# Gathering the experts' rows as quarter rows and turning them on VectorE

## The chip, the cores and the metric

The kernel runs on one core of one Trainium2 chip. The metric is device time in microseconds (us) of one execution. The profile calls TensorE's matmuls PE and its weight loads PEld, VectorE DVE, ScalarE ACT, GpSimd POOL and SyncE SP.

## The reference

Sliding-window attention (8 batches, 8 heads, 576 positions, head size 64, window 64) is followed by a mixture of experts in which each row uses one expert. A local gate decides whether a row takes its own best expert or keeps that of the row before it.

```python
# attention output, laid out as x: (8, 576, 512)
logits = np.einsum('bsd,de->bse', x, w_gate)          # 8 experts
local_gate = 1.0 / (1.0 + np.exp(-np.einsum('bsd,de->bse', x, w_local).squeeze(-1)))
...
            fresh_e = int(np.argmax(logits[b, s]))
            if s == 0 or local_gate[b, s] < 0.5:
                e = fresh_e
            else:
                e = prev_e if prev_e >= 0 else fresh_e
...
            h = np.maximum(x[b, s] @ w1[e], 0.0)      # 512 -> 1024
            out[b, s] = p[e] * (h @ w2[e])            # 1024 -> 512
```

All data are 32-bit floats; p is the softmax of the logits.

## The kernel before, in words

**Attention** (line 168 on) works through nine chunks of 512 rows, four pairs of heads each. The finished rows go by DMA to a table in DRAM, `xs` (line 106), one row of 512 values and 16 more columns (`PITCH`) that hold the row's weight p. The **Router** (line 702 on) sorts the 4608 rows by expert in two parts while other work runs: `first` for the rows of the first part, `second` for all. Its results are index tables: `idx` and `gx` say for every place in a block which row stands there, `ej` which expert a block has. The weights p go into the last columns of `xs` in `weigh`.

**Experts** (line 1131 on) then works block by block. A slot is 128 places. A *big* block has two slots (256 rows), a *single* block one, a *half* block 64 rows and a *quarter* block 32. The order is fixed in `run` (line 1498): three big blocks of the first part (-1, -2, -3), then

0, 1, S, 2, Q, 3, S, 4, 5, S, 6, Q, 7, S, 8, 9, H, 10, 11, 12, H

where a number is a big block, S a single, H a half and Q a quarter one. For each block:

- `rows` (line 1144) gathers its rows: for each slot one indirect DMA on GpSimd's queue takes 128 rows of 528 values from `xs` into a tile `xg` (line 1162). `weights` (line 1170) loads the expert's w1 and w2 by SP into a ring of four tiles. Both are done two blocks ahead.
- `turn` (line 1189) brings the 512 features onto the partitions: PE transposes each slot in four 128x128 pieces into PSUM (line 1196), DVE (in the first three blocks ACT) copies the result to `xt` (line 1197). For a big block `prepare` (line 1205) follows: DVE forms sums and differences of quarters of `xt` (`xs` in the profile, line 1231) and of w1 (`ws`, line 1220), for a Strassen scheme with seven products in place of eight.
- `big_hidden` (line 1249) makes the seven products of the first layer on PE (line 1268, 16 matmuls each), with copies on ACT and additions and relu on DVE and ACT (lines 1274 to 1280). `prepare2` forms sums of w2 on DVE, `halves` those of the hidden layer (`hs`).
- `big_result` (line 1302) makes the seven products of the second layer (line 1318, 8 matmuls each). DVE's `put` (line 1327) and ACT scale by p and write the two halves of y. `scatter` (line 1392) sends 128 rows of y to the output by an indirect DMA on GpSimd's queue. Each scatter waits until the one before it has landed, since both write the output.
- Single and half blocks use plain matmuls: `hidden` (line 1414) and `result` (lines 1442 and 1455). A quarter block is worked in hooks between the products of the big block ahead of it (`quarter`, line 1355), and the block after it is turned and prepared in the hooks behind.

The turn of block i+1 stands between the two layers of block i, on PE and on DVE. In this part PE, SP, DVE and ACT carry out their instructions in the order of the program (`manual_schedule`, line 1526); GpSimd's order is chosen by the framework's scheduler. Only the last scatter of block -2 is moved by hand (`later`), behind the gathers of block 0 (lines 1511 and 1528).

Of the kernel before, what the change touches and what calls it, by code (L numbers as in the profile page):

```python
# [35 lines left out]
PITCH = D + 16  # L36
# [47 lines left out]
def kernel(  # L84
# [12 lines left out]
    w1: bass.AP,  # L97
    w2: bass.AP,
# [7 lines left out]
    xs = dram.tile([N + 2, PITCH], F32, name="xs")  # L106
# [4 lines left out]
                gx=const.tile([P, NS], U32, name="gx"), gx1=const.tile([P, FIRST], U32, name="gx1"))  # L111
# [9 lines left out]
    moe = xs, w1, w2, out, tabs, lt, ident  # L121
    with ExitStack() as fast:
        ring = fast.enter_context(tc.tile_pool(name="ring", bufs=4))
        rt = Router(fast, tc, lt, xs, tabs, ident)
        ex = Experts(fast, tc, ring, *moe)
        zeros, n = ex.xp.tile([P, PITCH], F32, name="xg"), (ZR - T1) // HF
        nc.vector.memset(zeros[:HF], 0.0)
        for i in (ZR, N + 1):
            nc.gpsimd.dma_start(out=xs[i:i + 1, :], in_=zeros[:1])
        nc.gpsimd.dma_start(out=xs[T1:ZR, D:].rearrange("(c p) o -> p c o", p=HF),  # L130
                            in_=zeros[:HF, :n * (PITCH - D)].rearrange("p (c o) -> p c o", c=n))
        attention(tc, ring, kq, v3, v4, vt, vh, xs, lt, ok, wgs, wg2s, ident, rt, ex)
        ex.run(fast, rt, lambda ps: flag(nc, ps, ok, bad, tabs["ej"][:, NBLK:], rare, ident))
    if_rare = nc.values_load(rare[0:1, 0:1], min_val=0, max_val=1,  # L134
                             skip_runtime_bounds_check_because="the larger of two comparisons")
    with tc.If(if_rare > 0):
        if_bad = nc.values_load(bad[0:1, 0:1], min_val=0, max_val=1,
                                skip_runtime_bounds_check_because="the result of a comparison")
        with tc.If(if_bad > 0):
            careful(tc, q, k, v, xs, lt, wgs, ident)  # L140
# [27 lines left out]
def attention(ctx, tc, ring, kq, v3, v4, vt, vh, xs, lt, ok, wg, wg2, ident, rt, ex):  # L168
# [302 lines left out]
    for i, (sc, hp) in enumerate(units):  # L471
# [53 lines left out]
        if (sc, hp) == (NSC - 3, 3):  # L525
            ex.jobs = [ex.weights({}, -1, ("w1",), lambda: until(2, allr[:1, sc, hp, 0, :1]))]
            if side == ():
                ex.rows(ex.jobs[0], -1)
# [3 lines left out]
        if hp == HP - 1:  # L532
            if sc in GATED:
                nc.vector.tensor_reduce(lt[:, 4 * sc:4 * sc + 4, :], g.rearrange("p c h j e -> p c e (h j)"),
                                        axis=AX.X, op=Alu.add)
            nc.gpsimd.dma_start(out=xs[row_of(sc * SC):row_of(sc * SC) + SC, :D].rearrange("(c p) d -> p c d", p=P),
                                in_=x.rearrange("p c h j d -> p c (h j d)"))
# [11 lines left out]
def careful(ctx, tc, q, k, v, xs, lt, wgs, ident):  # L549
# [107 lines left out]
    def rows(st):  # L657
# [7 lines left out]
        nc.gpsimd.dma_start(out=xs[row_of(c * P):row_of(c * P) + P, :D], in_=x)  # L665
# [36 lines left out]
class Router:  # L702
# [9 lines left out]
    def __init__(self, ctx, tc, lt, xs, tabs, ident):  # L712
        self.nc, self.lt, self.xs, self.tabs, self.ident = tc.nc, lt, xs, tabs, ident
        self.pool = ctx.enter_context(tc.tile_pool(name="rt", bufs=1))
        self.tc, self.behind, self.links = tc, None, []
# [6 lines left out]
    def prepare(self):  # L722
# [17 lines left out]
        begin2 = tl("begin2", P, C)  # L740
# [4 lines left out]
        self.oh, self.rank = tl("oh", P, CV, E), tl("rank", P, CV, E)  # L745

# [5 lines left out]
        self.at = iota("posp", [P, 1], [[0, 1]], 1)  # L752
        self.cnt = [tl("cnt0", P, E), tl("cnt1", P, E)]
# [5 lines left out]
    def iota(self, name, shape, pattern, mul=0, base=0):  # L759
        i = self.tl(name + "_i", *shape, dt=I32)  # L760
        self.nc.gpsimd.iota(i, pattern=pattern, base=base, channel_multiplier=mul)
        f = self.tl(name, *shape)
        self.nc.vector.tensor_copy(f, i)
# [10 lines left out]
    def gate(self, part, psum):  # L774
# [111 lines left out]
        self.pt = tl("ptw", P, CMAX, PITCH - D)[:, :n]  # L886
        wide = [P, n, PITCH - D]
        vec.tensor_tensor(self.pt, last(pt).to_broadcast(wide), last(sm).to_broadcast(wide), op=Alu.mult)

    def weigh(self, part):  # L890

        chunks, xs = PART[part], self.xs
        c = chunks.start
        for a, b in ((0, T1), ) if not part else ((T1, ZR), (ZR, N)):
            for a, b in ((a, -(-a // P) * P), (-(-a // P) * P, b // P * P), (b // P * P, b)):
                if a >= b:
# [3 lines left out]
                    out=xs[row_of(a):row_of(a) + b - a, D:].rearrange("(c p) o -> p c o", p=p),  # L900
# [44 lines left out]
    def table(self, psum, cs, ns, lo, hi, idx, gx):  # L945
# [44 lines left out]
        else:  # L990
            vec.scalar_tensor_tensor(gx, at, float(ZR), at, Alu.is_ge, Alu.add)
        return at

# [33 lines left out]
    def second(self, psum):  # L1027
# [93 lines left out]
        for i in range(4):  # L1121
            vec.tensor_scalar(tabs["idxq"][i * QR:(i + 1) * QR], at[a, HF0:], 4.0, float(i), Alu.mult, Alu.add)

# [7 lines left out]
class Experts:  # L1131


    def __init__(self, ctx, tc, ring, xs, w1, w2, out, tabs, lt, ident):
        self.tc, self.nc, self.ring = tc, tc.nc, ring
        self.xs, self.w1, self.w2, self.out, self.tabs, self.ident = xs, w1, w2, out, tabs, ident
        self.xp = ctx.enter_context(tc.tile_pool(name="ex_x", bufs=2))
        self.jobs = []
# [5 lines left out]
    def rows(self, st, n):  # L1144
# [13 lines left out]
        elif n >= KINDS[1]:  # L1158
            st.update(half=n - KINDS[1], rows=HF)
        for s in slots:  # L1160
            x = (self.xp if n == -1 else self.xq).tile([P, PITCH], F32, name="xg")
            asked = self.nc.gpsimd.indirect_dma_start(  # L1162
                out=x, out_offset=None, in_=self.xs[:rows, :],
                in_offset=bass.IndirectOffsetOnAxis(ap=gx[:, s:s + 1], axis=0))
            st["x"].append(x)
            st["asked"] = asked
        st["pw"] = [x[:, D:D + 1] for x in st["x"]]
        return st

    def weights(self, st, n, names=("w1", "w2"), behind=lambda: None):  # L1170
# [4 lines left out]
        for name, w, a, b in (("w1", self.w1, DK, F), ("w2", self.w2, FK, D)):  # L1175
# [13 lines left out]
    def turn(self, st, quiet, later=False):  # L1189
# [3 lines left out]
        for i, x in enumerate(st["x"]):  # L1193
            tp = self.ps_t.tile([P, DK, P], F32, name="tp")
            for kk in range(DK):
                nc.tensor.transpose(tp[:, kk, :n], x[a, kk * P:(kk + 1) * P], self.ident[a, a])
            (nc.scalar.copy if quiet else nc.vector.tensor_copy)(xt[:, :, i * P:i * P + n], tp[:, :, :n])
        if n < P:
            st["pw"] = pw = self.wk.tile([P, 1], F32, name="pw")
            for i in range(P // n):  # L1200
                nc.vector.tensor_copy(pw[i * n:(i + 1) * n], x[a, D:D + 1])
# [100 lines left out]
    def big_result(self, st, hooks):  # L1302
# [47 lines left out]
        if "later" in st:  # L1350
            st["later"] = lambda: self.scatter(st, 1, y[1])
# [80 lines left out]
    def result(self, st, step, hooks=()):  # L1432
# [3 lines left out]
        if "half" in st:  # L1436
# [3 lines left out]
            for m in range(FK):  # L1440
# [5 lines left out]
            nc.gpsimd.indirect_dma_start(  # L1446
                out=self.out.rearrange("n (i d) -> (n i) d", i=2),
                out_offset=bass.IndirectOffsetOnAxis(ap=self.tabs["idxh"][:, s:s + 1], axis=0),
                in_=y[:, :w], in_offset=None, bounds_check=2 * N - 1, oob_is_err=False)
            step()  # L1450
            return
        for i, s in enumerate(st["slots"]):
# [8 lines left out]
            self.scatter(st, i, y)  # L1461
# [12 lines left out]
    def run(self, ctx, rt, last=None):  # L1474
# [36 lines left out]
        jobs[FB - 2]["later"] = None  # L1511
# [7 lines left out]
        for i, n in enumerate(order):  # L1519
            quiet = i < FB  # L1520
            if i == FB - 1:
                while side:
# [18 lines left out]
            if i == 1:  # L1541
                rt.behind = jobs[1]["last"]
            if i + 1 == len(order):
# [75 lines left out]
```

## Time and profile before

| what | value |
|---|---|
| three runs, median (lowest to highest) | 641.81 us (641.36 to 642.15) |
| the profiled execution's own time | 642.1 us |
| its span, first to last instruction | 640.0 us |
| granted TensorE clock, mean | 0.994 |
| DMA, mean over the span | 260 GB/s |
| scatters of whole rows (line 1394) | 36 |

The profile is of one execution. A row of a timeline gives the start in us from the span's start, the duration in us, the engine, the line, the operation with its tiles (out<-in), how many instructions were merged, and in brackets how long the engine had stood idle and what ended that. A row of a line's view gives counts and shortest/median/longest duration in ns.

### The profile page before, as it was taken

To read this page: it belongs to the slowest core of one execution; us is meant where nothing else is said; L and a number is where in the kernel's file an instruction comes from. 1 tells how busy PE (TensorE), PEld (TensorE's weight loads), DVE (VectorE), ACT (ScalarE), POOL (GpSimd) and SP (SyncE) were. 2 spreads that over 40 slices of the span, in tenths; PEclk is the share of its full clock that TensorE was granted. 3 is DMA by queue.
4 is the path that set the end of the run, shared out by engine and by line. 5 is a ranking of instruction groups with operands and counts; after the bars stand their busy time and mean duration, and the time that the engine had idled before them with its cause. 6 is when DMAs were issued, how large, how long until landed. Compare 5 with 4: busy or idle time off the path is not lost. (4 is left out here: it accounts for less than half of the span.)

```text
span 640.0 us, 14994 instructions
## 1 busy us (share of the span) xinstructions
PE 615.6 (96%) x6367; PEld 544.2 (85%) x6367; DVE 402.3 (63%) x752; ACT 200.6 (31%) x368; POOL 133.1 (21%) x132
## 2 busy tenths in 40 slices
PE   8889998899999999999999999999999999999995
PEld 7777777788889999978997999887997998899994
DVE  6676588879968775273654683362917752886730
ACT  3766765612572122113120312021211221213120
POOL 5422112430103202120302120211312022111101
PEclk9999998999999999999999999999999999999998
DMA  9999996969757645786958665769768556956501
GB/s 338 416 418 406 385 366 241 348 236 337 237 171 246 244 166 198 242 316 236 387 189 291 218 234 212 259 235 367 263 228 324 185 199 232 379 167 225 209 17 38
DMA packets 29318, 166.43 MB, mean 260 GB/s; under 512 B 8451, under 2 KB 9497, under 8 KB 20026
## 3 DMA queue, kind: packets, MB, share of 16 engines
q1 hardware_dynamic: 20394, 135.54, 58.4%
q0 software_dynamic: 8848, 29.85, 12.2%
q8 instruction: 52, 0.85, 0.5%
q14 instruction: 24, 0.20, 0.1%
HBM read 146.18 MB, written 19.59 MB: 259 GB/s over the span
## 5 line engine op out<-in xcount | busy, mean ns | idle before, releaser
L1394 POOL DMA_INDIRECT out_dram<-y,idx x36 | 41.1, 1141 | 339.1 <-DVE y L1327 196.5
L1318 PE MATMUL hp<-ws,hs 128*128 128x256 f32 x384 | 88.7, 380 | 0.0
L1318 PEld LDWEIGHTS hp<-ws,hs 128*128 128x128 f32 x384 | 72.6, 190 | 10.5 <-issue 0.8
L1268 PE MATMUL hp<-xs,ws 128*128 128x128 f32 x672 | 79.6, 275 | 0.0
L1268 PEld LDWEIGHTS hp<-xs,ws 128*128 128x128 f32 x672 | 77.3, 192 | 0.0
L1327 DVE SCALAR_TENSOR_TENSOR y<-hp,xg,kept 128x256 f32<-128x256 f32 x48 | 22.6, 482 | 74.2 <-issue 47.0
L1414 PE MATMUL hp<-xt,w 128*64 128x64 f32 (+2 forms) x640 | 66.2, 276 | 0.0
L1414 PEld LDWEIGHTS hp<-xt,w 128*128 128x128 f32 (+1 forms) x640 | 60.8, 170 | 4.1 <-issue 0.7
L1318 PE MATMUL hp<-w,h 128*128 128x256 f32 x256 | 61.1, 382 | 0.0
L1162 POOL DMA_INDIRECT xg<-xs,gx x40 | 50.3, 1258 | 45.6 <-issue 37.4
L1279 DVE TENSOR_TENSOR h<-hp,keep 128x512 f32<-128x512 f32 x42 | 28.6, 690 | 48.1 <-PE hp L1268 48.0
L1268 PEld LDWEIGHTS hp<-xt,w 128*128 128x128 f32 x448 | 53.2, 192 | 2.7 <-issue 1.3
L1268 PE MATMUL hp<-xt,w 128*128 128x128 f32 x448 | 54.7, 275 | 0.0
L1318 PEld LDWEIGHTS hp<-w,h 128*128 128x128 f32 x256 | 47.2, 190 | 6.3 <-issue 0.4
L431 PE MATMUL xo<-vb,p 128*64 128x74 f32 (+1 forms) x576 | 44.5, 230 | 7.0 <-issue 2.9
L416 ACT ACTIVATE p<-sp 128x512 f32<-128x512 f32 x72 | 39.2, 595 | 38.0 <-PE sp L385 35.9
L385 PEld LDWEIGHTS sp<-w 64*64 64x64 f32 x1296 | 38.7, 138 | 12.1 <-issue 8.5
L421 DVE TENSOR_TENSOR p<-p,mask 128x1024 f32<-128x1024 f32 x29 | 36.1, 1245 | 19.5 <-ACT p L416 19.3
L431 PEld LDWEIGHTS xo<-vb,p 128*64 128x64 f32 x576 | 38.9, 138 | 9.9 <-issue 4.4
L385 PE MATMUL sp<-w 64*64 64x128 f32 (+1 forms) x1296 | 43.8, 270 | 2.6 <-issue 1.5
L431 PE MATMUL xo<-va,p 128*64 128x74 f32 (+1 forms) x576 | 44.5, 230 | 1.2 <-issue 1.2
L1280 ACT ACTIVATE h<-h 128x512 f32<-128x512 f32 x42 | 26.3, 630 | 59.1 <-DVE h L1279 59.1
(280 smaller groups left out, 955.0 us busy)
## 6 DMA issues: line engine op xcount, KB each, us to landing
w<-in_w_dram SPq DMA_DIRECT2D x42, 2048.0 KB, 9.2
w<-in_kq_dram SPq DMA_DIRECT2D x17, 1024.0 KB, 8.7
w<-in_w_dram SPq DMA_DIRECT2D x24, 512.0 KB, 9.3
xs<-x POOLq DMA_DIRECT2D x9, 1024.0 KB, 9.5
va<-in_v_dram SPq DMA_DIRECT2D x5, 1184.0 KB, 8.9
vtt<-in_vt_dram SPq DMA_DIRECT2D x5, 1024.0 KB, 7.2
va<-in_v_dram SPq DMA_DIRECT2D x3, 1040.0 KB, 12.2
va<-in_v_dram SPq DMA_DIRECT2D x2, 520.0 KB, 6.8
```

Of the source, the lines that this page charges most:

```text
L385: nc.tensor.matmul(sp[j][c * WIN:(c + 1) * WIN, a:b], lhsT=kt[h, hp, block * WIN:(block + 1) * WIN], rhs=qt[h, hp, a:b], start=not biased, ...
L416: nc.scalar.activation(p[:, j], sp[j], Act.Exp, scale=DH ** -0.5)
L421: masked.append(nc.vector.tensor_tensor(p, p, m.to_broadcast([P, 2, SC]), op=Alu.mult))
L431: nc.tensor.matmul(xo[par * WIN:(par + 1) * WIN, j, s * VW:s * VW + n], lhsT=p[:, j, b * WIN:(b + 1) * WIN], rhs=w[:, s, 2 * hp + j, :n], ...
L1162: asked = self.nc.gpsimd.indirect_dma_start(out=x, out_offset=None, in_=self.xs[:rows, :], in_offset=bass.IndirectOffsetOnAxis(ap=gx[:, s: ...
L1268: nc.tensor.matmul(out[:, m, :], lhsT=a[:, kk, m * P:(m + 1) * P], rhs=b[:, kk, :], start=start and m + kk == 0, stop=stop and (m, kk) == ...
L1279: nc.vector.tensor_tensor(o, x, y, op=add)
L1280: nc.scalar.activation(o, x if y is None else o, Act.Relu)
L1318: nc.tensor.matmul(out, lhsT=a[:, m, :], rhs=b[:, m, :], start=start and m == 0, stop=stop and m == FK // 2 - 1, skip_group_check=True)
L1327: nc.vector.scalar_tensor_tensor(y[i][:, j * w:(j + 1) * w], x, pw[i], y2, Alu.mult, Alu.add)
L1394: self.nc.gpsimd.indirect_dma_start(out=self.out[:, :], out_offset=bass.IndirectOffsetOnAxis(ap=st["idx"][:, s:s + 1], axis=0), in_=y, in_ ...
L1414: nc.tensor.matmul(hp[a, i, :], lhsT=st["w1"][:, kk, m * P:(m + 1) * P][:, a], rhs=st["xt"][:, kk, :n], start=(kk == 0), stop=(kk == DK - 1))
```

## The change

- `xs` keeps the 512 values of a row alone; the weights p go to a table of their own, `xw`, of 16 columns.
- From block 1 on (the first three blocks and block 0 stay *plain*), a slot is gathered by four indirect DMAs in place of one. Gather m takes for 32 rows all four quarters: partition 32a+t gets quarter a (128 values) of row 32m+t. The indices for that, `g4`, are made once in a new step of the Router, `split`, with sixteen small matmuls.
- The weights p of every slot are fetched by one more gather, from `xw` into a tile `pws`, plain blocks included.
- `turn` of such a slot is one DVE transpose in 32x32 blocks from `xg` straight to `xt`, without PE and PSUM. Its order of features over the partitions differs from before, so these blocks load w1 from a second array `w1t`, whose rows are ordered to match.
- The last scatter of a block is held back (`late`) and issued by `flush` behind the gathers of the first slot of the next `rows`, or at the next block's start.
- In the first block after the Router, block 1's weights are loaded ahead, and its rows are gathered after the first layer of block -3, when `g4` is there.
- GpSimd is added to the engines that keep the program's order. The hooks of a quarter block come one product later. The Router's index tiles share one integer tile.

```diff
-    def rows(self, st, n):
+    def gather(self, out, table, idx, rows):
+        return self.nc.gpsimd.indirect_dma_start(
+            out=out, out_offset=None, in_=table[:rows, :],
+            in_offset=bass.IndirectOffsetOnAxis(ap=idx, axis=0))
+
+    def flush(self):
+
+        late, self.late = self.late, None
+        if late:
+            late()
+
+    def rows(self, st, n, plain=False):
...
+        st["plain"] = plain or n < 0
+        st["parts"] = range(2, 3) if "quarter" in st else range(st["rows"] // QR)
+        st["pw"] = []
         for s in slots:
-            x = (self.xp if n == -1 else self.xq).tile([P, PITCH], F32, name="xg")
-            asked = self.nc.gpsimd.indirect_dma_start(
-                out=x, out_offset=None, in_=self.xs[:rows, :],
-                in_offset=bass.IndirectOffsetOnAxis(ap=gx[:, s:s + 1], axis=0))
+            x = (self.xp if n == -1 else self.xq).tile([P, D], F32, name="xg")
+            if st["plain"]:
+                st["asked"] = self.gather(x, self.xs, gx[:, s:s + 1], rows)
+            else:
+                quarter = self.xs.rearrange("n (i d) -> (n i) d", i=4)
+                for m in st["parts"]:
+                    st["asked"] = self.gather(x[:, m * P:(m + 1) * P], quarter, tabs["g4"][:, m, s:s + 1], 4 * rows)
             st["x"].append(x)
-            st["asked"] = asked
-        st["pw"] = [x[:, D:D + 1] for x in st["x"]]
+            self.flush()
+        for s in slots:
+            pw = (self.pws if n == -1 else self.xq).tile([P, PW], F32, name="pws")
+            self.gather(pw, self.xw, gx[:, s:s + 1], rows)
+            st["pw"].append(pw[:, :1])
         return st
```

```diff
         for i, x in enumerate(st["x"]):
-            tp = self.ps_t.tile([P, DK, P], F32, name="tp")
-            for kk in range(DK):
-                nc.tensor.transpose(tp[:, kk, :n], x[a, kk * P:(kk + 1) * P], self.ident[a, a])
-            (nc.scalar.copy if quiet else nc.vector.tensor_copy)(xt[:, :, i * P:i * P + n], tp[:, :, :n])
+            o = xt[:, :, i * P:(i + 1) * P]
+            if st["plain"]:
+                tp = self.ps_t.tile([P, DK, P], F32, name="tp")
+                for kk in range(DK):
+                    nc.tensor.transpose(tp[:, kk, :n], x[a, kk * P:(kk + 1) * P], self.ident[a, a])
+                (nc.scalar.copy if quiet else nc.vector.tensor_copy)(o[:, :, :n], tp[:, :, :n])
+                continue
+            first, parts = st["parts"][0], len(st["parts"])
+            nc.vector.transpose(
+                o[:, :, :n].rearrange("p j (m t) -> p m j t", m=parts),
+                x[:, first * P:(first + parts) * P].rearrange("p (m j d) -> p m j d", m=parts, j=DK))
```

```diff
+    def split(self, psum):
+
+        nc, vec, gf = self.nc, self.nc.vector, self.gf
+        vec.tensor_scalar(gf, gf, 4.0, None, Alu.mult)
+        yield 1.0, True
+        places = psum()[:, :4 * NS].rearrange("p (m s) -> p m s", m=4)
+        for m in range(4):
+            for a in range(4):
+                nc.tensor.matmul(places[a * QR:(a + 1) * QR, m], lhsT=self.ident[:, m * QR:(m + 1) * QR], rhs=gf,
+                                 start=True, stop=True)
+        vec.tensor_scalar(self.tabs["g4"], places, self.group, None, Alu.add)
```

```diff
-                while side:
+                while side and not rt.ready:
                     step()
                 mark = last(self.ps_y.tile([P, D], F32, name="yp")) if last else None
 
-                ctx.enter_context(tc.manual_schedule(engines={ET.PE, ET.SP, ET.DVE, ET.Activation}))
-                st = self.rows({}, order[FB])
-                with tc.issue_after(st["asked"].ins):
-                    jobs[i - 1].pop("later")()
-                jobs.append(self.weights(st, order[FB]))
+                ctx.enter_context(tc.manual_schedule(engines={ET.PE, ET.SP, ET.DVE, ET.Activation, ET.Pool}))
+                jobs.append(self.weights(self.rows({}, order[FB], True), order[FB]))
+                jobs.append(self.weights({"plain": False}, order[FB + 1]))
                 if jobs[i]["fast1"]:
                     self.prepare(jobs[i])
-            if i + 2 > FB and i + 2 < len(order):
+            elif i + 2 > FB and i + 2 < len(order):
                 jobs.append(self.fetch(order[i + 2]))
+            self.flush()
+            if FB - 1 <= i < len(order) - 1:
+                jobs[i]["later"] = True
...
+            if i == FB - 1:
+                while side:
+                    step()
+                self.rows(jobs[FB + 1], order[FB + 1])
...
-                hooks = one, turned, two, (lambda: None), (lambda: self.turn(after, False, True)), \
+                hooks = (lambda: None), one, turned, two, (lambda: self.turn(after, False, True)), \
                     (lambda: self.prepare(after))
```

More of the change, by code (lines that the diff above doesn't have):

```diff
@@ L119 @@
     bad, rare = const.tile([1, 1], I32, name="bad"), const.tile([1, 1], I32, name="rare")
-    moe = xs, w1, w2, out, tabs, lt, ident
+    xs = xs, xw
+    moe = xs, (w1, w1t), w2, out, tabs, lt, ident
     with ExitStack() as fast:
@@ L125 @@
         ex = Experts(fast, tc, ring, *moe)
-        zeros, n = ex.xp.tile([P, PITCH], F32, name="xg"), (ZR - T1) // HF
+        zeros, n = ex.xp.tile([P, D], F32, name="xg"), (ZR - T1) // HF
         nc.vector.memset(zeros[:HF], 0.0)
         for i in (ZR, N + 1):
[L129 to L132, printed above, removed]
+            nc.gpsimd.dma_start(out=xs[0][i:i + 1, :], in_=zeros[:1])
+            nc.gpsimd.dma_start(out=xw[i:i + 1, :], in_=zeros[:1, :PW])
+        nc.gpsimd.dma_start(out=xw[T1:ZR, :].rearrange("(c p) o -> p c o", p=HF),
+                            in_=zeros[:HF, :n * PW].rearrange("p (c o) -> p c o", c=n))
+        attention(tc, ring, kq, v3, v4, vt, vh, xs[0], lt, ok, wgs, wg2s, ident, rt, ex)
         ex.run(fast, rt, lambda ps: flag(nc, ps, ok, bad, tabs["ej"][:, NBLK:], rare, ident))
@@ L139 @@
         with tc.If(if_bad > 0):
[L140 removed]
+            careful(tc, q, k, v, xs[0], lt, wgs, ident)
             with ExitStack() as slow:
@@ L525, in attention @@
         if (sc, hp) == (NSC - 3, 3):
-            ex.jobs = [ex.weights({}, -1, ("w1",), lambda: until(2, allr[:1, sc, hp, 0, :1]))]
+            ex.jobs = [ex.weights({"plain": True}, -1, ("w1",), lambda: until(2, allr[:1, sc, hp, 0, :1]))]
             if side == ():
@@ L759, in iota @@
     def iota(self, name, shape, pattern, mul=0, base=0):
-        i = self.tl(name + "_i", *shape, dt=I32)
+        n = 1
+        for x in shape[1:]:
+            n *= x
+        i = self.tl("iota_i", P, P, dt=I32)[:shape[0], :n]
         self.nc.gpsimd.iota(i, pattern=pattern, base=base, channel_multiplier=mul)
         f = self.tl(name, *shape)
-        self.nc.vector.tensor_copy(f, i)
+        self.nc.vector.tensor_copy(f.rearrange("p a b -> p (a b)") if len(shape) == 3 else f, i)
         return f
@@ L1122, in second @@
             vec.tensor_scalar(tabs["idxq"][i * QR:(i + 1) * QR], at[a, HF0:], 4.0, float(i), Alu.mult, Alu.add)
+        self.ready = True
+        yield 0.0, True
+        yield from self.split(psum)
 def quarters(t, rows, cols):
@@ L1135, in __init__ @@
         self.tc, self.nc, self.ring = tc, tc.nc, ring
-        self.xs, self.w1, self.w2, self.out, self.tabs, self.ident = xs, w1, w2, out, tabs, ident
+        self.xs, self.xw = xs
+        self.w1, self.w2, self.out, self.tabs, self.ident = w1, w2, out, tabs, ident
         self.xp = ctx.enter_context(tc.tile_pool(name="ex_x", bufs=2))
+        self.late = None
+        self.pws = ctx.enter_context(tc.tile_pool(name="ex_pw", bufs=2))
         self.jobs = []
@@ L1349, in big_result @@
         nc.scalar.activation(y[1][:, :w], px, Act.Copy, scale=pw[1])
-        if "later" in st:
-            st["later"] = lambda: self.scatter(st, 1, y[1])
+        if st.pop("later", None):
+            self.late = lambda: self.scatter(st, 1, y[1])
         else:
@@ L1445, in result, with store @@
             nc.scalar.activation(y[:, :w], yp[:, :w], Act.Copy, scale=st["pw"])
[L1446 to L1449, printed above, removed]
+            def store():
+                nc.gpsimd.indirect_dma_start(
+                    out=self.out.rearrange("n (i d) -> (n i) d", i=2),
+                    out_offset=bass.IndirectOffsetOnAxis(ap=self.tabs["idxh"][:, s:s + 1], axis=0),
+                    in_=y[:, :w], in_offset=None, bounds_check=2 * N - 1, oob_is_err=False)
+            if st.pop("later", None):
+                self.late = store
+            else:
+                store()
             step()
@@ L1460, in result @@
             nc.scalar.activation(y, yp, Act.Copy, scale=st["pw"][i])
-            self.scatter(st, i, y)
+            if i + 1 == len(st["slots"]) and st.pop("later", None):
+                self.late = lambda: self.scatter(st, i, y)
+            else:
+                self.scatter(st, i, y)
             step()
```

45 lines of the change are left out of this document (28 added, 17 removed).

## The prediction

> **What bounds the kernel now.** I read the busy times, then stage by stage, then the order of events at the places where a block's rows are turned.
>
> ```profile
> PE 615.6 (96%) x6367; PEld 544.2 (85%) x6367; DVE 402.3 (63%) x752; ACT 200.6 (31%) x368; POOL 133.1 (21%) x132
> ```
>
> ```profile
> 0.00:127.00 127.00, 112.75 (x2637) 93.62 (x2637) 91.69 (x227) 78.51 (x132) 40.46 (x53) 0.99 0.95 364
> ...
> 242.00:613.00 371.00, 370.05 (x2758) 332.15 (x2756) 213.48 (x295) 79.21 (x144) 70.31 (x59) 1.00 0.69 250
> ```
>
> The second fence is the table by stage (stretch, length, busy PE, weight loads, DVE, ACT, POOL, clock, DMA share). From 242 to 613 us, where nearly all turns to be changed lie, PE is busy 370.05 of 371 us at full clock. So there a PE instruction that goes shortens the kernel by its spacing, unless something else then comes late. The next ones to look at are DVE (213 us) and Pool (70 us), which is given more work.
>
> **What is removed.** The first fence is the line that turns rows on PE, and the copy from PSUM behind it; then come the places where it stands, in order of time.
>
> ```profile
> L1196 PE MATMUL tp<-ident,xg x160: 220/272/328, 131.2 to 613.1; 128*128 128x128 f32 x144, 32*128 32x32 f32 x8, 64*128 64x64 f32 x8
> L1197 DVE COPY xt<-tp x34: 285/682/692, 206.3 to 615.1; 128x512 f32<-128x512 f32 x30, 128x128 f32<-128x128 f32 x2, 128x256 f32<-128x256 f32 x2
> ```
>
> Four blocks (-1, -2, -3 and 0) keep this way: 8 slots, 32 transposes. The other 20 blocks lose 128: 28 full slots of four (24 of twelve two-slot blocks, 4 of single-slot ones), 2 half and 2 quarter slots of four small ones. Their modelled 272 ns overlap, so I price by spacing.
>
> ```profile
> 391.40 0.60 PE L1196 MATMUL tp<-ident,xg 128*128 128x128 f32 x4
> 391.84 1.89 PE L1318 MATMUL hp<-w,h 128*128 128x256 f32 x8
> ```
>
> Four take 0.44 us, 0.11 each. The four turns from a big block to a single one give 4 x 0.44 = 1.8 us: no preparation follows them on DVE.
>
> From a big block to the next big one (five times: 0-1, 4-5, 8-9, 10-11, 11-12) it is different:
>
> ```profile
> 229.25 0.69 DVE L1220 TENSOR_TENSOR hs<-h 128x512 f32<-128x512 f32 x1 [0.69 <-ACT h L1280]
> 229.44 1.04 PE L1196 MATMUL tp<-ident,xg 128*128 128x128 f32 x8
> 230.32 1.89 PE L1318 MATMUL hp<-w,h 128*128 128x256 f32 x8
> 231.78 1.28 DVE L1197 COPY xt<-tp 128x512 f32<-128x512 f32 x2
> 234.57 1.22 DVE L1220 TENSOR_TENSOR ws<-w 128x1024 f32<-128x1024 f32 x1
> 238.10 1.22 DVE L1220 TENSOR_TENSOR ws<-w,ws 128x1024 f32<-128x1024 f32 x1
> 239.24 0.87 DVE L1327 SCALAR_TENSOR_TENSOR y<-hp,xg,kept 128x256 f32<-128x256 f32 x2
> 240.68 1.89 PE L1318 MATMUL hp<-ws,h 128*128 128x256 f32 x8
> ```
>
> PE loses 0.88 us (229.44 to 230.32). But the last product (240.68) adds into the PSUM tile that the second of the two operations at 239.24 reads, and these end at 240.11. DVE's chain from 229.25 to there is unbroken and doesn't wait for the transposes: the copies begin after `hs`, long after PE was done. So PE can come forward by 240.68 - 240.11 = 0.57 us less a semaphore; I take 0.5. Five times 0.5 = 2.5 us, and 0.4 us each go into a new wait of PE for DVE.
>
> From a single or half slot to a big block (five times) DVE has more time:
>
> ```profile
> 345.69 1.04 PE L1196 MATMUL tp<-ident,xg 128*128 128x128 f32 x8
> 346.50 1.28 DVE L1197 COPY xt<-tp 128x512 f32<-128x512 f32 x2
> 346.56 7.03 PE L1455 MATMUL yp<-w,h 128*128 128x512 f32 x16
> 360.85 0.69 DVE L1279 TENSOR_TENSOR h<-hp,keep 128x512 f32<-128x512 f32 x1 [2.15 <-PE hp L1268]
> ```
>
> DVE idles 2.15 us for PE before the first addition of the next block, so PE's 0.87 us come out whole: 5 x 0.87 = 4.35 us.
>
> The two quarter blocks, each with the big one behind it:
>
> ```profile
> 294.92 0.43 PE L1196 MATMUL tp<-ident,xg 32*128 32x32 f32 x4
> 295.28 1.99 PE L1318 MATMUL hp<-w,h 128*128 128x256 f32 x8
> ...
> 308.68 1.04 PE L1196 MATMUL tp<-ident,xg 128*128 128x128 f32 x8
> 309.56 1.89 PE L1318 MATMUL hp<-w,hs 128*128 128x256 f32 x8
> ```
>
> 0.36 + 0.88 = 1.24 us, twice 2.5 us. The hooks move one product later, which changes the order alone. The two half slots lie between 0.36 and 0.44; at 0.4 they give 0.8 us. Sum removed: 1.8 + 2.5 + 4.35 + 2.5 + 0.8 = 12.0 us.
>
> **What is added on DVE.** One turn of 128x512 for each copy of 128x512; no row shows one. The copies are its nearest rows: 285 ns for 128 columns and 682 for 512, 1.03 ns an element. From below I allow a quarter of that less, from above half the rate, 0.53 us more. I take the copy's time, as both move the same elements through the same engine. "VectorE: DVE Perf Modes" of the Trainium skill, section "The three transpose paths", gives 311 ns for a 128x128 turn in bf16; an estimate from it is 25 ns more than the copy, some 0.25 us over the five places where DVE decides. No run here shows it yet.
>
> **What is added on PE.**
>
> ```profile
> 303.24 1.96 PE L1381 MATMUL yp<-w,qt 128*32 128x128 f32 x64
> ```
>
> Sixteen small matmuls in `split`, with a few DVE operations beside them. Between 0.03 (four column groups side by side, as the quarter block's 64 in 1.96 us) and 0.11 each (the transposes above): 0.5 to 1.8 us; I take 1.0.
>
> **What is added and moved on Pool.** A big block now asks 10 gathers (8 of quarter rows, 2 of weights) for 2; a single one 5, a half 3, a quarter 2. After block 0 that is 150 for 32.
>
> ```profile
> L1394 POOL DMA_INDIRECT out_dram<-y,idx x36 | 41.1, 1141 | 339.1 <-DVE y L1327 196.5
> L1162 POOL DMA_INDIRECT xg<-xs,gx x40 | 50.3, 1258 | 45.6 <-issue 37.4
> ```
>
> ```profile
> L1162 POOL DMA_INDIRECT xg<-xs,gx x40: 942/988/1954, 117.1 to 575.3; - x40
> DMA to landing us min/median/max: 3.7/7.2/10.5
> ```
>
> ```profile
> 216.25 1.01 POOL L1394 DMA_INDIRECT out_dram<-y,idx  x1 [13.32 <-DVE y L1327]
> 219.52 0.95 POOL L1162 DMA_INDIRECT xg<-xs,gx  x1 [0.30 <-issue]
> 219.54 1.23 DVE L1231 TENSOR_TENSOR ws<-w 128x1024 f32<-128x1024 f32 x1
> 225.25 1.01 POOL L1394 DMA_INDIRECT out_dram<-y,idx  x1 [4.79 <-DMA out_dram<-y,idx]
> 241.72 1.01 POOL L1394 DMA_INDIRECT out_dram<-y,idx  x1 [15.45 <-DVE y L1327]
> ```
>
> A gather describes 128 pieces before and after, so I keep its time: 1.26 + 0.30 of gap = 1.56 us, a scatter 1.44. A big block costs Pool 15.6 + 2.9 = 18.5 of its 25.5 us (216.25 to 241.72). A scatter waits for the one before it to land (216.25 to 225.25); four gathers now fill 6.2 of those 9 us. Queued behind it are the second slot's gathers; they still go out by about 233 (226.6 and four of 1.56), and the turn that needs them is one block after the one at 231.78, near 257. So in the big blocks the gathers are hidden. If that cover goes, DVE waits for rows with all its later work behind it.
>
> The narrow place is after a quarter block: between its big block's first scatter (314.00) and the turn at 346.50 stand 13 gathers and 2 scatters, 23.2 us, and a landing of 4 to 7: rows by 341 to 344, 2 to 5 us to spare. With every gather at its longest (2.25 with the gap) it would be some 4 us late, and the 2.15 us of DVE at 360.85 would take part of that.
>
> ```profile
> 199.39 1.02 POOL L1394 DMA_INDIRECT out_dram<-y,idx  x1 [2.05 <-DMA out_dram<-y,idx]
> 203.98 1.04 PE L1196 MATMUL tp<-ident,xg 128*128 128x128 f32 x8
> ```
>
> Once, the moved scatter is in the way: block 0's second gather now stands behind the scatter at 199.39, so it goes out at 200.7 and lands at 204.4 (3.7, the shortest) or somewhat later, while PE wants it from 204.4. Cost 0 to 1 us; I take 0.5. At the start two small DMAs come ahead of Pool's first index. DVE's mask is 1 us later at most; until 127 us the DMA share is 0.95 and PE is busy 112.75 of 127, so other work covers it: 0, up to 1. The shared index tile makes Pool and DVE take turns in the same stretch: the same cover, the same price.
>
> **Sum.** 12.0 - 1.0 - 0.5 = 10.5 us. The profiled run took 642.1 us (span 640.0 and 2.1 around it), 0.3 over the median of 641.81: 631.6 against the profiled run, 631.3 against the median.
>
> **Rivals.**
> 1. *A turn runs at half the copy's rate.* Each pair takes 1.06 us more. The five big-to-big turns then cost 0.56 each (-2.8); the quarter places keep 0.2 each (0.4); of the 4.35 about 3.4 stays; 2.6 of the single and half turns stay whole. 3.6 - 1.5 = 2.1: 639.7. For it: the turn has no row. Against it: nothing in the rows speaks of a half rate. 0.15.
> 2. *The turn is so quick that DVE nowhere decides.* It needs 0.4 us off a pair of 1.28. Then all PE time comes out: 28 x 0.44 + 0.8 + 0.7 = 13.8, less 1.5: 629.5; 628.5 with the cheapest `split` and no stall. 0.12.
> 3. *Slower: Pool becomes the bound.* A gather that meets a DVE operation with two inputs in SBUF waits for it; the longest took 1954 ns. Pool's list from 204.5 (after the two weight gathers of block 0) to the last row gather is 150 gathers and about 31 scatters (45 us), and the last turn's rows must be there by 615. It decides from (615 - 4 - 204.5 - 45)/150 = 2.4 us a gather. At 2.5 the last rows come 13 us late: 655. Against it: the mean is 1.56, and the gather at 219.52 took 0.95 beside a 1.23 us operation that began with it, so it isn't held for all of such an operation. "SBUF — State Buffer" of the Trainium skill, section "Who interferes with whom", says that the later of the two blocks fully until the first is done; by that rule Pool would have only DVE's free time, and this rival would be the forecast; the gather at 219.52 doesn't agree. 0.10.
> 4. *The savings are eaten in small waits* (rows 3 us late at the narrow places, DVE's order in the attention stage): 641.8. 0.04.
>
> The forecast has 0.59. Faster or slower is counted from 0.2%, 1.3 us, about what a measurement of this kernel can tell from no change. Faster: 0.59 + 0.15 + 0.12 = 0.86, less 0.02 for the slow end of the first rival: 0.84. Same: 0.04. Slower: 0.12, with 0.02 for stalls that the fourth undercounts. The range takes the forecast's own bounds (629.5 to 634) and the first two rivals: 628.5 to 640.
>
> **What would show it.** Right: L1196 down to 32; PE waits of about 0.4 us for `y` before the last product of blocks 0, 4, 8, 10 and 11, and none before a big block's first product; turns of about 0.68 us; Pool near 295 us busy (166 gathers at 1.26, 40 scatters at 1.14, 40 of the rest) with gathers still near 1.26; PE near 603. Wrong: turns of 1.2 us; DVE or PE waiting for gathers of quarter rows, above all behind the quarter blocks; gathers at 2 us or more on the mean; a longer stretch before 127 us.

## The result, and the profile after

| kernel | median | lowest to highest |
|---|---|---|
| before, beside it | 642.14 us | 641.36 to 644.29 (6 runs) |
| after | 633.41 us | 631.75 to 635.46 (6 runs) |

The ratio is 0.9854, 95% interval [0.9834, 0.9874]: 8.7 us less where 10.5 were forecast. That is one occasion, whose chip is not on record. On two later ones, on the chips numbered 9 and 5, the same changed kernel took 681 us beside 644 to 645 us for the kernel before. The experiments below are mostly about that, and they end with its cause only half known. In the tables the ratios leave out runs over 1.5% longer than the fastest of the same kernel, and none is given where too few are left; medians are of all runs.

The profiled execution of the first occasion took 635.46 us, the longest of its six; its span is 633.2 us. Its busy times, and two stretches of its table by stage (columns as in the prediction):

```profile
PE 605.1 (96%) x6271; PEld 532.2 (84%) x6271; DVE 403.8 (64%) x757; ACT 200.8 (32%) x368; POOL 271.1 (43%) x261
```

```profile
0.00:127.00 127.00, 112.29 (x2598) 92.69 (x2599) 91.82 (x228) 78.47 (x132) 42.20 (x58) 0.99 0.94 359
...
242.00:606.00 364.00, 362.10 (x2660) 323.04 (x2659) 216.94 (x302) 79.68 (x144) 186.21 (x166) 1.00 0.70 254
```

PE has shed 10.5 us of work and is still busy nearly all of the time (362.10 of 364), while Pool's busy time has doubled. The instructions that gather and turn rows:

```profile
L1176 POOL DMA_INDIRECT xg<-xs,g x118: 941/948/2007, 207.2 to 575.6; - x118
L1249 PE MATMUL tp<-ident,xg x32: 272/273/328, 134.2 to 208.7; 128*128 128x128 f32 x32
L1253 DVE STREAM_TRANSPOSE xt<-xg x32: 303/684/705, 235.7 to 606.9; 128x512 f32<-128x512 f32 x28, 128x128 f32<-128x128 f32 x2, 128x256 f32<-128x256 f32 x2
...
DMA to landing us min/median/max: 2.5/3.4/8.4
```

32 transposes are left on PE. A turn takes 684 ns on DVE, as the copy did (682). A gather of quarter rows keeps Pool for 948 ns in the median, and its rows land sooner than the whole ones did. The turn from block 0 to block 1, DVE and then PE:

```profile
235.70 1.30 DVE L1253 STREAM_TRANSPOSE xt<-xg 128x512 f32<-128x512 f32 x2
...
242.11 1.22 DVE L1279 TENSOR_TENSOR ws<-w,ws 128x1024 f32<-128x1024 f32 x1
243.24 1.26 DVE L1386 SCALAR_TENSOR_TENSOR y<-hp,pws,kept 128x256 f32<-128x256 f32 x3
```

```profile
242.00 1.89 PE L1377 MATMUL hp<-w,hs 128*128 128x256 f32 x8
244.17 1.99 PE L1377 MATMUL hp<-ws,h 128*128 128x256 f32 x8 [0.28 <-DVE y L1386]
```

The last product stands still for 0.28 us until DVE has read the PSUM tile that it adds to: the new wait of the prediction, in its place. By the starts of the products it costs 0.55 us, where 0.4 was forecast.

### The profile page after: what moved, and what is told of

The parts are those of the page before. It is cut to its first block, busy times and chain, and to the rows that moved or that the text cites. A ratio compares the mean times of both kernels' runs of the same rounds, so it can differ in the third digit from the quotient of the medians.

```text
span 633.2 us, 14966 instructions
## 1 busy us (share of the span) xinstructions
PE 605.1 (96%) x6271; PEld 532.2 (84%) x6271; DVE 403.8 (64%) x757; ACT 200.8 (32%) x368; POOL 271.1 (43%) x261
## 5 line engine op out<-in xcount | busy, mean ns | idle before, releaser
L1176 POOL DMA_INDIRECT xg<-xs,g x118 | 132.9, 1126 | 36.0 <-issue 34.1
L1386 DVE SCALAR_TENSOR_TENSOR y<-hp,pws,kept 128x256 f32<-128x256 f32 x48 | 22.1, 480 | 63.2 <-issue 38.0
L435 PE MATMUL xo<-vb,p 128*64 128x74 f32 (+1 forms) x576 | 46.2, 235 | 8.2 <-DVE x L445 3.5
L1176 POOL DMA_INDIRECT pws<-xw,gx x40 | 45.4, 1134 | 12.2 <-issue 11.9
L435 PEld LDWEIGHTS xo<-vb,p 128*64 128x64 f32 x576 | 40.6, 143 | 11.0 <-issue 3.8
L435 PE MATMUL xo<-va,p 128*64 128x74 f32 (+1 forms) x576 | 46.3, 235 | 0.6 <-issue 0.6
```

Of the source, the lines that this page charges most:

```text
L435: nc.tensor.matmul(xo[par * WIN:(par + 1) * WIN, j, s * VW:s * VW + n], lhsT=p[:, j, b * WIN:(b + 1) * WIN], rhs=w[:, s, 2 * hp + j, :n], ...
L1176: return self.nc.gpsimd.indirect_dma_start(out=out, out_offset=None, in_=table[:rows, :], in_offset=bass.IndirectOffsetOnAxis(ap=idx, axis=0))
L1386: nc.vector.scalar_tensor_tensor(y[i][:, j * w:(j + 1) * w], x, pw[i], y2, Alu.mult, Alu.add)
```

## The experiments

Each group of four ran on one chip (9, then 5, then 10), with the kernel before beside it. On chip 10 the changed kernel itself was not run unedited.

| kernel | median (lowest to highest) | before | ratio and 95% interval |
|---|---|---|---|
| `ctrl`: after, unedited | 681.10 (675.41 to 689.93) | 644.92 | 1.0587 [1.0541, 1.0633] |
| `pe_back` | 693.93 (689.75 to 700.85) | 644.92 | 1.0739 [1.0704, 1.0775] |
| `turn2` | 699.10 (675.84 to 705.04) | 644.92 | none |
| `order2` | 675.57 (668.34 to 692.39) | 644.92 | 1.0389 [1.0346, 1.0431] |
| `ctrl2`: after, unedited | 681.59 (672.03 to 691.58) | 644.42 | 1.0483 [1.0406, 1.0560] |
| `whole` | 642.96 (641.14 to 645.60) | 644.42 | 0.9970 [0.9953, 0.9988] |
| `before_q` | 785.67 (782.22 to 790.70) | 644.42 | 1.2183 [1.2115, 1.2251] |
| `no_hold` | 700.67 (698.42 to 706.01) | 644.42 | 1.0888 [1.0830, 1.0946] |
| `pool_plain` | 687.39 (684.25 to 690.48) | 644.85 | 1.0682 [1.0626, 1.0738] |
| `sp_plain` | 645.62 (643.18 to 647.40) | 644.85 | 1.0012 [0.9994, 1.0030] |
| `pool_work` | 673.77 (672.34 to 674.83) | 644.85 | 1.0448 [1.0419, 1.0478] |
| `spaced` | 654.31 (652.67 to 655.29) | 644.85 | 1.0159 [1.0131, 1.0186] |

### The changed kernel again: `ctrl`

> The changed kernel once more, nothing edited. Theory A (the shortfall against the forecast is run-to-run: a moment of lower granted clock in the attention stage and a longer end after the last product, both by chance in the profiled run): the time stays within 631.7 to 635.5 us, but in this profile the first expert product begins less than 2 us later than the 133.41 us of the kernel before (136.43 in the first profile), the stretch from there to the last product's end stays within 0.3 us of 487.7 us, and the end behind it comes back to 7.1 us or lands elsewhere between 7 and 9. Rival B (a standing cost of the new start DMAs and the shared index tile): the first expert product is again at 136.4 us, 3 us late.

Neither theory had this in view: 681 us, 48 more than at first. The first expert product starts at 136.18 us, in the first profile at 136.43, so what is new lies behind it. The stretch from 202 to 222 us, first in the profile of the first occasion, then in this one:

```profile
202.00:222.00 20.00, 20.00 (x155) 18.48 (x156) 14.67 (x22) 4.39 (x8) 15.69 (x15) 1.00 0.54 181
```

```profile
202.00:222.00 20.00, 12.68 (x92) 10.60 (x81) 4.28 (x7) 2.02 (x4) 13.29 (x14) 0.84 0.19 55
```

PE, DVE and ACT all do less, while Pool asks one gather after the other (13.29 us busy in 14 instructions). What PE, DVE and ACT do there:

```profile
211.93 1.09 PE L1249 MATMUL tp<-ident,xg 128*128 128x128 f32 x8
212.85 0.81 PE L1377 MATMUL hp<-w,h 128*128 128x256 f32 x3
214.01 1.10 PE L1377 MATMUL hp<-w,h 128*128 128x256 f32 x3 [0.35 <-issue]
216.13 0.59 PE L1377 MATMUL hp<-w,h 128*128 128x256 f32 x2 [1.02 <-issue]
```

```profile
204.10 1.95 PE L1327 MATMUL hp<-xt,ws 128*128 128x128 f32 x16
208.46 3.68 PE L1327 MATMUL hp<-xs,w 128*128 128x128 f32 x16 [2.41 <-DVE h L1338]
216.16 0.69 DVE L1338 TENSOR_TENSOR h<-hp,keep 128x512 f32<-128x512 f32 x1 [7.75 <-remote]
221.87 0.60 ACT L1339 ACTIVATE h<-hp 128x512 f32<-128x512 f32 x1 [4.36 <-remote]
```

Two things are wrong. Eight matmuls of one product, between which PE waits for nothing that the profile shows ("issue"), take from 212.85 to 216.7 us, where such eight take 1.89 us elsewhere. And results are taken up late ("remote": the profile names no instruction of this core that ended the wait): the addition at 216.16 reads the product of 204.10, which had ended by 206.1, the relu at 221.87 the one of 208.46, which had ended by 212.1. In the first profile the same addition begins at 206.31, as its product ends (206.27). A slower clock is not what stretches the eight matmuls: from 211.9 to 216.7 us the granted clock is 0.99. Pool itself isn't slowed: its gathers take 0.94 us there, as at first. The rule of the Trainium skill, "SBUF — State Buffer", section "Who interferes with whom", that PE and ACT never wait on anyone because only DVE and GpSimd share ports, holds in the first profile and doesn't explain this one.

### PE's time put back: `pe_back`

```diff
+            tp = self.ps_t.tile([P, DK, P], F32, name="tp")
+            for kk in range(DK):
+                nc.tensor.transpose(tp[:, kk, :n], self.ident[a], self.ident[a, a])
             nc.vector.transpose(
```

> The changed kernel with PE's four transposes put back in front of every VectorE turn (of the identity, into a PSUM tile nobody reads), so PE has its old time and VectorE, Pool and the order keep the new. Theory A (all of the gain is PE time): 12.0 us more than the changed kernel by the forecast's sum, 12.7 by the landmarks of the two traces, so about 646 us, above the 641.8 us of the kernel before. Rival B (the late scatter and the earlier landings give part of the gain themselves): 8 us more or less than that, at most 642 us.

12.8 us more than `ctrl` by the medians, some 10 by the ratios (0.0152 x 645). The absolute times were expected for the first occasion and don't apply here. The difference does: about what PE's transposes are worth by the sum (12.0), so no large part of the gain came from elsewhere. With runs that spread over 11 to 15 us it is no finer than that.

### Each turn done twice: `turn2`

```diff
-            nc.vector.transpose(
+            for _ in range(2):
+                nc.vector.transpose(
```

> Every VectorE turn done twice, the second one a copy of the first: 0.68 us more of VectorE per slot, 1.37 for a two-slot block. Theory A (VectorE decides at the five big-to-big turns only, and has 1.28 us to spare behind single and half slots): 5 x 1.37 = 6.9 us there, 5 x 0.1 behind the singles, up to 0.5 at each quarter block: 7 to 8.5 us more than the changed kernel, and PE's wait for y before the last product of those five blocks grows from 0.3 to 1.7 us. Rival B (VectorE bounds the whole expert stage): 28 x 0.68 = 19 us more. Rival C (VectorE decides nowhere): 0 to 1 us more.

The time settles nothing: its runs spread over 29 us and overlap with those of `ctrl`. The place that was forecast does show it; PE before the last product of block 0:

```profile
252.76 1.89 PE L1378 MATMUL hp<-w,hs 128*128 128x256 f32 x8
256.43 0.92 PE L1378 MATMUL hp<-ws,h 128*128 128x256 f32 x3 [1.78 <-DVE y L1387]
```

1.78 us for 0.28, and 1.77 at three of the other four big-to-big turns: there DVE decides, as forecast. At the two quarter places PE waits 1.1 us each for DVE's `ws`, where up to 0.5 was expected. Behind single blocks PE waits for no turn.

### DVE's order at those five places: `order2`

```diff
+        do(ops[:3] if rest else ops)              # the sums over w1
+        return (lambda: do(ops[3:])) if rest else None
...
-            hooks = (step, ) * 6
+            hooks = (step, ) * 4 + (rest or step, step)
```

> VectorE's order changed at the five big-to-big turns: the fourth sum over w1 (1.22 us) is asked for after the first two operations that write y, not before. Theory A (PE's last product waits for those two because all four sums stand ahead of them): 0.55 us less at each of five places, 2.7 us less than the changed kernel, no wait for y left. Rival B (the 0.3 us of PE's wait comes of something else, the PSUM tile or ScalarE): no difference, within 0.5 us.

5.5 us less than `ctrl` by the medians, 12.8 by the ratios; but its runs, from 668 to 692 us, cover nearly all of those of `ctrl`, from 675 to 690, so the time doesn't measure the gain. The waits show more. PE's waits for y behind 190 us, in `ctrl` and in `order2` (total, times, longest):

```profile
PE hp L1377 <- DVE y L1386: 3.6, 4, 1.5
```

```profile
PE hp L1388 <- DVE y L1397: 1.3, 2, 0.9
```

All four waits of `ctrl` stand at big-to-big turns, two of 0.28 us, as in the first profile, and two of 1.52. In `order2` such a turn keeps one of 0.38; the one of 0.90 is at a turn to a single block. So the order is a cause of that wait; the 2.7 us were not measured.

### What makes it slow: `ctrl2`, `whole`, `before_q`

> The changed kernel a third time, nothing edited. It took 633.4 us at first and 681.1 us on another occasion, on another chip, beside 642.1 and 644.9 us for the kernel before. In the slow profile all engines stop together while Pool asks a row of gathers (PE 12.7 of 20 us busy from 202 to 222 us, against 20.0 of 20 in the first profile). If that is a matter of the chip or the occasion it comes out near one of these two values again; if it is chance from run to run, it comes out spread between them.

681.6 us on chip 5. So it is no chance from run to run: two values, and the later two occasions agree. Chip and occasion can't be told apart by these runs.

```diff
-                for m in st["parts"]:
-                    st["asked"] = self.gather(x[:, m * P:(m + 1) * P], quarter, tabs["g4"][:, m, s:s + 1], 4 * rows)
+                st["asked"] = self.gather(x, self.xs, gx[:, s:s + 1], rows)
```

> The changed kernel with one gather of whole rows per slot in place of the four of quarter rows (so the turned rows are in a wrong order: the gather by quarters is left out); VectorE's turns, the separate gather of the weights and the late scatter stay. Theory A (the many gathers stop the other engines where the kernel is slow): 631 to 634 us wherever it runs, about 10 us below the kernel before. Theory B (the turn or the late scatter is what is slow there): as slow as the changed kernel beside it, 670 to 690 us where that takes 681.

642.96 us, where theory A had 631 to 634: 39 of the 48 us are gone with the gathers, not all. Part of the rest is the same disturbance. One row is left in which Pool asks eight transfers, one every 1.3 us (201.4 to 211.2 us), and there an addition is 2.6 us late and PE waits for it:

```profile
PE hp L1325 <- DVE h L1336: 3.7, 3, 3.3
```

Theory A is right in the main, some 6 us stay unexplained, and DVE's turn is not what is slow.

```diff
             st["asked"] = asked                        # in the kernel before
+            if n > 0:
+                w, more = PITCH // 4, self.xp.tile([P, PITCH], F32, name="xg")
+                for m in range(4):
+                    self.nc.gpsimd.indirect_dma_start(out=more[:, m * w:(m + 1) * w], ...)
```

> The kernel before with four more gathers of quarter rows per slot behind each gather (into a buffer that nobody reads), from block 1 on; PE, VectorE and the scatters are untouched. Theory A (the many gathers stop the other engines): where the changed kernel takes 681 us this takes 30 to 45 us more than the kernel before, although nothing waits for these gathers; where the changed kernel takes 633 it takes 0 to 2 more. Theory B: 0 to 2 us more everywhere.

141 us more where theory A had 30 to 45, from gathers that nobody waits for (in this profile PE, DVE and ACT wait for no DMA behind 127 us), in a kernel that has neither the turn nor the late scatter. PE and Pool in this run:

```profile
337.38 0.59 PE L1325 MATMUL hp<-w,h 128*128 128x256 f32 x1 [0.33 <-issue]
339.48 1.29 PE L1325 MATMUL hp<-w,h 128*128 128x256 f32 x2 [1.51 <-issue]
341.58 0.58 PE L1325 MATMUL hp<-w,h 128*128 128x256 f32 x1 [0.82 <-issue]
343.68 0.59 PE L1325 MATMUL hp<-w,h 128*128 128x256 f32 x1 [1.51 <-issue]
```

```profile
342.06 0.94 POOL L1170 DMA_INDIRECT xg<-xs,gx  x1 [0.30 <-DMA xg<-xs,gx]
343.31 0.95 POOL L1170 DMA_INDIRECT xg<-xs,gx  x1 [0.30 <-DMA xg<-xs,gx]
```

Pool asks every 1.25 us; PE's matmuls of one product follow at 2.1 us, where 0.22 is usual. The granted clock is 0.50 from 337 to 351 us; half the clock would make 0.44 of the 0.22, so it is a small part of this. The product ahead of them, and the relu that reads it:

```profile
331.88 3.78 PE L1275 MATMUL hp<-xs,w 128*128 128x128 f32 x16 [6.16 <-DVE h L1286]
```

```profile
396.90 0.60 ACT L1287 ACTIVATE h<-hp 128x512 f32<-128x512 f32 x1 [35.05 <-remote]
```

The relu comes 61 us behind its product, after Pool's unbroken row has ended at 389.7 us.

### The late scatter: `no_hold`

```diff
-            if FB - 1 <= i < len(order) - 1:
-                jobs[i]["later"] = True
```

> The changed kernel with a block's last scatter asked for at once, not among the next gathers (blocks 0 and on). By the forecast the order of scatters and gathers is hidden: within 1.5 us of the changed kernel beside it. Rival: Pool then waits for the landing of the scatter before, with the gathers behind it: 2 to 5 us more, at the places behind a quarter block.

19 us more than `ctrl2`, where the forecast was 1.5 at most and the rival had 2 to 5. One part is the rival's: DVE waits three times for rows whose gathers came late, which it does nowhere in `ctrl` and `ctrl2`:

```profile
DVE xt L1253 <- DMA xg<-xs,g: 18.4, 3, 7.1
```

How much of this the kernel pays is open. The other part may be the rows of transfers: some are of 11 here where in `ctrl` a held scatter, for which Pool has to wait, cuts them into 5 and 7. But the longest row has 22, and in `ctrl2` 26. So the split of the 19 us is not shown. On the first occasion this kernel wasn't run.

### Whose transfers, and at what pace: `pool_plain`, `sp_plain`, `pool_work`, `spaced`

The first three put, in the place of the four gathers of `before_q`:

```diff
+  self.nc.gpsimd.dma_start(out=more[:, m * w:(m + 1) * w], in_=self.xs[:P, m * w:(m + 1) * w])   # pool_plain
+  self.nc.sync.dma_start(out=more[:, m * w:(m + 1) * w], in_=self.xs[:P, m * w:(m + 1) * w])     # sp_plain
+  self.nc.gpsimd.memset(more, 0.0)                                                               # pool_work
```

> The kernel before with four plain transfers per slot (128 pieces of 528 bytes each, from block 1 on, into a buffer that nobody reads) asked by Pool where the run with four more gathers had gathers. That run took 141 us more than the kernel before, with PE busy for 15 of 70 us while Pool asked one gather after the other. Theory A (it is Pool's making of transfers, indexed or not, that holds up the other engines): 50 to 150 us more. Theory B (only the indexed ones do it): 0 to 5 us more.

42.5 us more, but not in the way of `before_q`. PE's two longest waits, and a place where Pool asks 24 transfers in one row:

```profile
PE tp L1200 <- DMA xg<-xs,gx: 23.1, 1, 23.1
PE hp L1322 <- DVE y L1331: 9.5, 3, 6.6
```

```profile
273.71 12.93 POOL L1170 DMA_DIRECT2D xg<-xs  x24 [4.71 <-DMA xg<-xs]
283.18 1.95 PE L1272 MATMUL hp<-xs,w 128*128 128x128 f32 x16
285.16 0.60 ACT L1284 ACTIVATE h<-hp 128x512 f32<-128x512 f32 x1 [0.43 <-PE hp L1272]
301.95 0.88 DVE L1331 SCALAR_TENSOR_TENSOR y<-hp,xg,kept 128x256 f32<-128x256 f32 x2 [6.38 <-DMA out_dram<-y,idx]
302.48 3.78 PE L1322 MATMUL hp<-ws,h 128*128 128x256 f32 x8 [6.56 <-DVE y L1331]
```

The first wait is for real rows, whose gather stood behind the added transfers in Pool's queue. The second is for DVE, which wants `y` tiles whose scatters stood there too. Inside the row PE keeps its pace (16 matmuls in 1.95 us), and the relu begins 0.03 us after its product. No wait of this profile behind 127 us ends with "remote". Behind a wait eight matmuls take up to 3.8 us for 1.9, so PE's busy time is 7.1 us longer. With the two waits (0.3 of the second were there before) that is 39.4 of the 42.6 us that the span has grown. So these 42.5 us are a matter of Pool's order, not of theory A: plain transfers made by Pool, one every 0.54 us, slow no other engine here. That leaves theory B, though its 0 to 5 us left out the queue.

> The same four plain transfers per slot asked by SP, on the queue that brings the weights, and none added on Pool. Theory A (Pool's making of transfers is the cause): 0 to 5 us more than the kernel before. Theory C (the many small pieces and their landings are the cause, whoever asks for them): 50 to 150 us more, as with the gathers.

Nothing, 0.8 us within its interval:

```profile
202.00:222.00 20.00, 20.00 (x129) 18.50 (x128) 16.09 (x23) 4.75 (x9) 4.81 (x5) 1.00 0.64 216
222.00:270.00 48.00, 48.00 (x328) 45.11 (x327) 25.46 (x36) 11.28 (x21) 7.66 (x7) 1.00 0.62 219
```

The same bytes, asked by SP, are free, though the profile counts 18432 packets more in SP's queue, and 4096 more in Pool's where Pool asks. So it is not the small pieces or their landings. With `pool_plain` what is left is the gathers by index that Pool makes one behind the other.

> The kernel before with four Pool fills of a 128x512 tile per slot in place of the four gathers: Pool is as busy, but no transfer is added. Theories A, B and C: 0 to 5 us more than the kernel before (some of it from VectorE and Pool sharing their way to SBUF). Theory D (any unbroken work of Pool holds up the others): 50 us or more.

29 us more, against all of A, B and C, but in another way. Pool and DVE:

```profile
173.34 26.96 POOL L1170 MEMSET xg<- 128x528 f32 x56
```

```profile
174.80 25.66 DVE L967 TENSOR_SCALAR colh<-one,posp 128x540 bf16<-128x540 bf16 x1
202.87 0.35 DVE L967 TENSOR_SCALAR colh<-one,posp 128x540 bf16<-128x540 bf16 x1
```

One bf16 operation of the Router, 0.35 us otherwise, is held for 25.66 us until 56 fills are through; the hidden sums behind it on DVE are late, and PE waits 25.9 us for them. "SBUF — State Buffer", same section, says that such an operation can run in a mode in which it and a GpSimd instruction lock each other out for the whole of one instruction; here an unbroken row of them kept DVE out for the row. From 222 to 270 us PE is busy for 47.75 of 48, with Pool busy for 41.53, so Pool's work alone doesn't make PE stumble: theory D isn't borne out.

```diff
+        if gap is not None:
+            self.nc.gpsimd.memset(gap, 0.0)      # in gather, from block 1 on
```

> The changed kernel with a Pool fill of a 128x512 tile behind every gather from block 1 on, so that the gathers don't follow on each other at once. Theory E (an unbroken row of gathers does the harm, since the first few of a row pass unharmed in the slow profiles): 635 to 665 us beside about 681 for the changed kernel on such a chip. Theory F (each gather costs the same wherever it stands, some 0.36 us): 675 to 690 us.

654.3 us: with more work on Pool it is 27 us faster than the unspaced kernel was on chips 9 and 5. Since that kernel was not run on chip 10, its own profile has to show that this chip disturbs it too, and it does in one place. Block 0's gathers have no fills, and four transfers follow there at 1.3 us (200.77 to 204.58); the relu that is due at 205.9 comes 4.4 us late:

```profile
203.94 1.95 PE L1331 MATMUL hp<-xs,w 128*128 128x128 f32 x16
210.28 0.60 ACT L1343 ACTIVATE h<-hp 128x512 f32<-128x512 f32 x1 [2.35 <-remote]
```

Behind that place no wait of PE, DVE or ACT ends with "remote", and a gather follows every 1.65 us:

```profile
202.00:222.00 20.00, 17.74 (x102) 15.27 (x102) 12.67 (x20) 3.20 (x7) 17.86 (x21) 1.00 0.54 177
222.00:270.00 48.00, 47.73 (x329) 44.67 (x329) 28.90 (x39) 12.25 (x22) 29.71 (x36) 1.00 0.56 202
```

```profile
375.98 0.48 DVE L1390 SCALAR_TENSOR_TENSOR y<-hp,pws,kept 128x256 f32<-128x256 f32 x1
386.01 0.88 DVE L1390 SCALAR_TENSOR_TENSOR y<-hp,pws,kept 128x256 f32<-128x256 f32 x2 [9.55 <-DMA out_dram<-y,idx]
```

That fits theory E. Whether it is the pace or the other work between the gathers can't be told. Over half of what is left (the span is 17.7 us longer than in the first profile) is one wait: DVE wants a `y` tile whose held-back scatter stands behind gathers and fills on Pool, and PE waits 9.9 us for DVE. That is the third rival of the prediction, Pool as the bound, brought about by the fills.

## Why the prediction was right, and where it was not

**By its own steps, on the first occasion**, from the starts of the products in the two profiles:

| step | forecast | measured |
|---|---|---|
| big to single, four | 1.8 | 1.8 (0.44 each) |
| big to big, five | 2.5 | 1.6 (0.88 gained, 0.55 given back each) |
| single or half to big, five | 4.35 | 4.7 |
| quarter places, two | 2.5 | 3.5 |
| half slots, two | 0.8 | 1.2 |
| sum | 12.0 | 12.7 |
| `split` on PE | -1.0 | -0.9 |
| stall behind the moved scatter | -0.5 | 0 |
| attention stage | 0 | -1.4 |
| end, behind the last matmul | 0 | -1.9 |
| net | 10.5 | 8.5 |

The medians give 8.7. The mechanism was right: PE's time comes out whole where DVE has time to spare, and DVE's order takes its part at five places. The turn has the copy's duration, so the first two rivals fall. That the sum is met within 0.7 us is in part luck: the big-to-big turns gave 0.9 us less, the quarter places 1.0 more. There the prediction said that the later hooks change the order alone; but PE's wait for the quarter block's `xt` (0.23 us at 297.50 and at 434.00 before) is gone with it, which is part of the 1.0.

What was mis-sized is the two zeros. The attention stage: the first expert product begins at 135.4 us in the mean of nine profiles with the changed Router (133.9 to 136.4) and at 133.9 in five with the old one (133.4 to 134.3), so the "0, up to 1 each" for the start DMAs and the shared index tile was 1.4. In the first profile it was 3.0, which may be why the profiled run was the longest. The end: from the last matmul to the end of the span are 7.1 to 7.5 us in the three kernels with as few Pool transfers as before, and 8.7 to 10.8 us in the eleven with more. The prediction didn't look there at all, and the cause of the longer end is open. The expectation for `ctrl` that both were chance was wrong.

**On the later chips** the forecast, with its whole range, was wrong. The step that failed is "so in the big blocks the gathers are hidden". It asked whether Pool and DVE have the time, and they have. It took for granted that what Pool does costs the other engines nothing, and the third rival too had only Pool's own delay in it. `before_q` shows on chip 5 that an unbroken row of gathers made by Pool slows PE and makes signals between engines late, though nobody waits for the gathers. On chip 10 the same bytes without an index did neither, asked by SP or by Pool. `spaced` shows late signals at its one unspaced row alone: one gather every 1.65 us with a fill between them avoided them, one every 1.3 us without did not.

**Open** is which resource this is, and why the first occasion had none of it: there Pool asked 33 transfers in one row (450.0 to 495.4 us), and PE stood for 0.24 us, as it did at the same place before. Open too is whether it goes with the chip or with the occasion. The slow profiles hold no landings of the gathers, so it can't be read from them whether these were late. Nor can it be told whether the recording of the profile has a part in it.

## What to carry to other kernels

Work moved off the engine that bounds a kernel comes out whole only as far as the next engine's order allows, and that can be read beforehand, place by place. But a queue that gets four times the transfers is not free because it has time left: ask it of the chip with transfers that nobody waits for, added to the old kernel, before building on it, and on more than one chip. Where Pool must make many gathers by index, let them not follow on each other at once, or let SP ask for what needs no index.

## What the runs showed of the hardware

- On one chip gathers made by Pool every 1.25 us slowed PE to a matmul in 2.1 us (granted clock 0.50) and delayed a relu by 61 us (`before_q`). On two chips the changed kernel was slow and showed the same signs (a relu 9.7 us late in `ctrl`); on the first occasion it did not.
- The same bytes without an index cost 0.8 us asked by SP, within the error (`sp_plain`). Asked by Pool they cost 42.5 us, by what stood behind them in its queue; a relu in a row of 24 such transfers was 0.03 us behind its product (`pool_plain`).
- A DVE operation in bf16 (128x540, 0.35 us) was kept out for 25.66 us by 56 fills of Pool without a gap.
- A DVE transpose of 128x512 32-bit values in 32x32 blocks takes 684 ns, as long as the copy of them out of PSUM.
- The stretch behind the last matmul took 8.7 to 10.8 us in the eleven profiles in which Pool made more transfers, 7.1 to 7.5 in the three others.
